# The state update of block 1 moved from step 8 to step 7, and half of the second raw weights loaded in the place of a w load

## The chip, the cores and the metric

The kernel runs on one core of one Trainium2 chip. The metric is device microseconds of one execution, the median of the runs shown. A profile is one further execution, with its own time.

## The reference

Two layers stand one behind the other. The first is an RWKV-6 attention over 4 batches, 8 heads, 768 time steps and a head width of 48. For each head a 48x48 state is carried along time:

```python
for t in range(S):
    kt, vt, rt, wt = (k[:, :, t], v[:, :, t], r[:, :, t], w[:, :, t])
    cur = np.einsum('bhd,bhe->bhde', u[None] * kt, vt)
    y[:, :, t] = np.einsum('bhd,bhde->bhe', rt, state + cur)
    state = wt[:, :, :, None] * state + np.einsum('bhd,bhe->bhde', kt, vt)
```

The second is a dense block on the 3072 tokens of 384 features that come out: `h = x @ w_in` (384 to 2048), `g = h - tanh(h)`, `out = g @ w_out` (2048 to 384), in 32-bit floats.

## The kernel before

The 3072 tokens are cut into eight blocks of 384 (`NB`), two for each batch. A block has six chunks of 64 tokens, and its 8 heads stand as four pairs, worked on in two halves of two pairs (`h1`, pairs 2 and 3, and `h2`, pairs 0 and 1). The recurrence is computed by chunks: products of w forwards (`before`, tile `pre`) and backwards (`behind`, tile `post`), scores within a chunk (`own` and `earlier`, L481), the sums of k and v of each chunk (`update_1`, L562, on TensorE from the turned keys `ks`), the states along the chunks (`update_2`, L574, eleven operations on VectorE for block 1), and the result from states (L664) and scores (L682).

The attention of block 0 is computed in a prologue, `boot`. After it the main loop runs over the blocks, and for each block over 16 steps f (`NF`), one for each 128 of the 2048 hidden features. Step f does the first matmul of block i (`first`, L828, into the PSUM tile hp), copies it on ScalarE (`h`, L831), makes g of it (`slight`, L857 to L861, with `product`, L834), and adds the second matmul of an earlier step (L905 in block 0, three steps behind; L952 in the later blocks). Between these the steps carry the attention of the next block: `plan(i)` says in which step each phase stands (`phases`: TensorE's matmuls, and the VectorE operations that follow them, which are put into the list `behind`) and each preparation (`before`: names such as product_u or held). The order on every engine is the order of the code. For block 0, step f's VectorE work is the list `ops`: conversions, the square, the rest of step f-1, of `behind` the first six, and what is left over waits for the next step.

The phases and block 1's scores share two PSUM tiles, `ps_a.both` (att in the profile), which take turns: turn, update, earlier and the results all use them.

The weights come as raw 64-bit numbers, 16 loads of 768 KB (tile raw, 5 buffers, issued on SP's queue), and are put together as 32-bit floats in four operations: three on ScalarE (L263) and one on VectorE (L267). `boot` converts the first two and most of the third. In block 0 `PIECES[f]` says how many of ScalarE's pieces step f does. `begin_behind(ins, dma)` makes a load wait until an instruction is done. SP issues in order: in `boot` the first raw weights, then w of block 1 for its pairs 2 and 3 (`later.load("w", UP, UP)`), the second raw weights behind the result of the first half, the rows of xT (`fill_holes`), the third and fourth, and w for pairs 0 and 1. At the end of `boot` the first of these w is read by `later.prepare("behind 2")` on VectorE.

Of the kernel before, what the change touches and what calls it, by code (L numbers as in the profile page):

```python
# [38 lines left out]
I32 = mybir.dt.int32  # L39
# [22 lines left out]
UP = 2  # L62
# [3 lines left out]
DM = H * D  # L66
# [6 lines left out]
RAWS = 5  # L73
LAG = 2
LAST = 5
PIECES = 0, 0, 2, 3, 3, 3, 3, 3, 4, 3, 3, 4, 4
UNITS = [(0, 0), (0, 1)] + [u for j in range(NF // 2 - 2) for u in ((1, j), (0, j + 2))] + [(1, NF // 2 - 2),
                                                                                      (1, NF // 2 - 1)]
LATE = 3
# [46 lines left out]
def kernel(  # L126
# [12 lines left out]
    nc = tc.nc  # L139
# [103 lines left out]
    ones = const.tile([P, 1], F32, name="ones", tag="ones")  # L243
    nc.gpsimd.memset(ones, 1.0)

    def load_weights(n, queue):
        part, j = UNITS[n]
        raw = conv.tile([P, 2 * DM, 2], I32, name="raw", tag="raw")
        src = weights[part, j].bitcast(I32).rearrange("p (n two) -> p n two", two=2)
        return part, j, raw, queue.dma_start(out=raw, in_=src)  # L250

    def convert(part, j, raw, _):

# [752 lines left out]
    def plan(i):  # L1006


        formed_w = {}
        if i == 0:  # L1010
            phases = {6: ("turn",), 8: ("update",), 10: ("earlier",), 13: ("result 1",)}
            before = {2: ("behind 0", "take_whole 0"), 3: ("times_behind 2",), 4: ("times_behind 0",),
                      5: ("before 2",), 6: ("before 0",), 7: ("times_before",), 8: ("product_u", "held"), 9: ("bound 2",), 10: ("product_r", "bound 0"),
                      11: ("product_sum",), 12: ("diagonal_in 2", "diagonal_in 0")}
            ahead = {}
            loads = {f: "weights" for f in (0, 1, 3, 4, 5, 6, 7, 8, 9, 10)}
            loads.update({2: "next r", 11: "w", 13: "k", 14: "r"})
            loads = {f: [name] for f, name in loads.items()}
            loads[3] += ["v", "row"]
            loads[4] += ["tokens k"]  # L1020
            loads[9] += ["tokens r"]
        else:
            phases = {3: ("split 2 0",), 4: ("earlier", "split 2 1", "turned 2", "split 0 01"), 5: ("turned 0",),
                      6: ("join 2 0",), 7: ("join 2 1",), 8: ("join 2 2",), 9: ("join 0 02",), 10: ("update",),
                      12: ("result 1",)}
            before = {0: ("times_behind 2",), 1: ("times_behind 0",), 3: ("times_before", "held"),
                      5: ("product_u",), 6: ("product_r",), 7: ("product_sum",), 8: ("diagonal_in 2",),
                      9: ("diagonal_in 0",)}
            ahead = {10: ("bound 2", "bound 0"), 11: ("behind 2", "take_whole 2"), 12: ("behind 0", "take_whole 0"),
                     13: ("before 2",), 15: ("before 0",)}  # L1030
            loads = {1: ["v"], 3: ["tokens k"], 4: ["tokens r"], 7: ["w"], 9: ["k"], 11: ["r"]}
        if i == 1:
            phases = {4: ("split 2 0",), 5: ("split 2 1", "turned 2"), 6: ("split 0 01",),
                      7: ("earlier", "turned 0", "join 2 0"), 8: ("join 2 1",), 9: ("join 2 2", "join 0 01"),
                      10: ("join 0 2",), 11: ("update",), 13: ("result 1",)}
            before = {0: ("behind 2", "take_whole 2", "bound 2"), 1: ("behind 0", "take_whole 0"),
                      2: ("times_behind 2",), 3: ("before 2", "bound 0"), 4: ("times_behind 0",), 5: ("before 0",),
                      6: ("times_before", "held"), 7: ("product_u",),
                      9: ("product_r", "product_sum", "diagonal_in 2"), 10: ("diagonal_in 0",)}
            ahead = {12: ("bound 2",), 13: ("behind 2", "take_whole 2"), 14: ("bound 0",)}  # L1040
            loads = {1: ["v"], 4: ["tokens k"], 6: ["tokens r"], 9: ["w"], 11: ["k"], 12: ["r"]}
            formed_w = {2: (0, 1), 7: (2, 3, 4, 5), 9: (6,), 10: (7, 8), 11: (9,), 12: (0, 1), 13: (2, 3, 4, 5, 6),
                        14: (7, 8, 9)}
        elif i == 2:
            phases.update({3: (), 4: ("split 2 0",), 5: ("earlier", "split 2 1", "turned 2", "split 0 01"),
                           6: ("turned 0", "join 2 0")})
            before = {0: ("behind 0", "take_whole 0", "times_behind 2"), 1: ("times_behind 0",), 2: ("before 2",),
                      3: ("before 0",), 4: ("times_before", "held"), 5: ("product_u",), 7: ("product_r",),
                      8: ("product_sum",), 9: ("diagonal_in 2", "diagonal_in 0")}
            loads = {1: ["v"], 3: ["tokens k"], 5: ["tokens r"], 8: ["w"], 10: ["k"], 11: ["r"]}  # L1050
        return phases, before, ahead, loads, formed_w
# [3 lines left out]
    manual.enter_context(tc.manual_schedule(engines={PE, SP, DVE, ACT}))  # L1055
    raws = []

    def more_weights(queue):
        raws.append(load_weights(more_weights.n, queue))
        more_weights.n += 1  # L1060
        return raws[-1][-1]

# [22 lines left out]
    def boot(ps, pair, blk, later):  # L1085
        h1, h2 = HALVES
        blk.tiles["w"] = states0
        for name, p0, n in (("w", h1 + 1, 1), ("w", h1, 1), ("k", h1, UP), ("r", h1, UP), ("w", h2, UP)):
            blk.load(name, p0, n)
        blk.load_v(h1, UP)  # L1090
        blk.load("k", h2, UP)
        blk.load_v(h2, UP)
        blk.load("r", h2, UP)

        both = (h1, h1 + 1), (h2, h2 + 1)
        blk.behind(h1 + 1, 1)
        blk.behind(h1, 1)
        blk.take_whole(h1, UP)
        blk.totals_by_column(h1)
        nc.scalar.copy(out=later_ident, in_=ident)  # L1100
        blk.before(h1, UP)
        blk.times_behind(h1, UP)
        blk.times_u(h1, UP)
        own = blk.own(ps, h1, ahead=8, late=7)
        blk.turn_1(ps, h1)
        blk.times_before(h1, UP)
        earlier = blk.earlier(ps, h1)
        begin_behind(blk.opened, more_weights(nc.sync))
        later.load("w", UP, UP)
        blk.behind(h2, UP)  # L1110
        blk.take_whole(h2, UP)
        first_a, first_b = convert(*raws.pop(0))
        own()
        blk.turn_2(h1)
        blk.totals_by_column(h2)
        blk.update_half(pair, h1)
        blk.times_behind(h2, UP)
        blk.times_u(h2, UP)
        blk.turn_1(ps, h2)
        blk.turn_2(h2)  # L1120
        earlier()
        blk.results(ps, halved=True)
        blk.result("from_scores", both[0])
        run(blk.states_half(h1))
        blk.result("from_states", both[0], True)
        begin_behind(blk.done, more_weights(nc.sync))
        blk.before(h2, UP)
        own = blk.own(ps, h2)
        blk.update_half(pair, h2)
        updated = blk.done  # L1130
        blk.times_before(h2, UP)
        blk.result_out((3,), nc.scalar.copy)
        blk.result_out((2,))
        earlier = blk.earlier(ps, h2, ahead=2)
        run(first_a)
        blk.fill_holes([nc.sync, nc.gpsimd])
        begin_behind(updated, more_weights(nc.sync))
        more_weights(nc.sync)
        later.load("w", 0, UP)
        second_a, second_b = convert(*raws.pop(0))  # L1140
        third_a, third_b = convert(*raws.pop(0))
        run(second_a)
        more_weights(nc.sync)
        own()
        onwards = blk.states_half(h2)
        blk.results(ps, halved=True)
        busy(blk.yp[0][:, 0], 3)
        blk.result("from_states", both[1])
        earlier(1, 1)
        earlier(0, 1)  # L1150
        later.load("k")
        more_weights(nc.sync)
        for p in reversed(both[1]):
            blk.result("from_scores", (p,), True, more=True)
        run(onwards)
        run(first_b)
        blk.result_out((1,), nc.scalar.copy)
        blk.result_out((0,), nc.vector.tensor_copy)
        run(third_a[:2])
        run(second_b)  # L1160
        later.prepare("behind 2")
        later.prepare("take_whole 2")
        blk.held(0, NPAIR)
        return [(third_a[2], third_b)]
# [32 lines left out]
    for i, blk in enumerate(blocks):  # L1197
# [9 lines left out]
        for f in range(NF):  # L1207
# [22 lines left out]
            elif now == 1:  # L1230
                ops = rest + square + converting(pieces, 3)
            elif not i:
                ops = extra + square + rest[:1] + behind[:6] + spare + rest[1:]
            elif forming:
                ops = between(rest, forming[:2]) + square + formed + forming[2:]
                ops = (between(ops, behind) if len(behind) > 2 else ops + behind) + spare
# [3 lines left out]
                ops = between(rest + formed, behind + spare)  # L1240
            for op in ops:
                op()
            rest, behind, formed, forming, held_back = later_ops, [] if i else behind[6:], [], held_back, []
            extra = [] if i else made_up
            if f < few[i]:
                q = f // 2
# [153 lines left out]
```

## Time and profile before

| | |
|---|---|
| median of 3 runs | 556.11 us (556.03 to 556.36) |
| the profiled execution | 554.57 us |
| its span, first to last instruction | 552.9 us |
| TensorE busy | 537.1 us (97%) |
| VectorE busy | 459.1 us (83%) |
| ScalarE busy | 403.9 us (73%) |
| mean granted TensorE clock | 0.996 |
| `boot`, up to the first L828 | 0 to 24.4 us |
| block 0's 16 steps on TensorE | 24.4 to about 97 us |

The times in the profile count from the first instruction of the span. In its rows a line such as L574 is the line of the kernel file; PE is TensorE, PEld its weight load, DVE VectorE, ACT ScalarE, POOL GpSimd, SP the engine that issues loads. In a list of waits, a row gives who waited for whom, the sum in us, how often, and the longest. In the chain of waits, a row gives start, length and the engine and line that the end of the program hung on. In a timeline, a row gives start, length, engine, line, operation, out<-in and count, and in brackets idle time before it and what ended it. In the list of DMA issues, the last number is the time from issue to landing. A matmul of 32-bit floats stands as two records.

### The profile page before, as it was taken

Reading aid. Unit: us, or ns where it says so; the run is one execution under the profiler, and the core shown is the slowest. Engines: PE = TensorE matmul, PEld = TensorE weight load, DVE = VectorE, ACT = ScalarE, POOL = GpSimd, SP = SyncE. Lnnn points to the kernel's source line nnn. Section 1 sums busy time; section 2 is a strip of 40 time slices with the busy share of each in tenths; the row PEclk is TensorE's granted clock in tenths of the full one; section 3 lists DMA queues with packets and bytes.
Section 4 is the critical chain, followed back from the end, with each engine's and each line's share of the span. In section 5 each row is a group of like instructions: output and inputs, shape, how many; then the busy total and the mean of one; then the engine's idle time right before and its main releaser. Section 6 shows DMA issues by size and latency. Waiting matters only on the chain.

```text
span 552.9 us, 13991 instructions
## 1 busy us (share of the span) xinstructions
PE 537.1 (97%) x5644; PEld 401.5 (73%) x5644; DVE 459.1 (83%) x942; ACT 403.9 (73%) x814; POOL 5.3 (1%) x33
## 2 busy tenths in 40 slices
PE   6899799999999999999999999999999999999996
PEld 3656566677777787878778787777878787787874
DVE  7899979899988899789897799869797897557563
ACT  5799966898668886588766886588865885666561
POOL 1100000000000000000000000000000000000000
PEclk9999999999999999999999999999999999999999
DMA  7898614243302632135211732126222420100101
GB/s 237 300 410 293 218 59 126 87 116 87 117 12 85 107 116 93 59 96 143 82 55 46 142 116 63 52 87 159 61 94 58 91 55 3 56 0 1 43 2 46
DMA packets 53461, 56.29 MB, mean 102 GB/s; under 512 B 21520, under 2 KB 51344, under 8 KB 53392
## 3 DMA queue, kind: packets, MB, share of 16 engines
q1 hardware_dynamic: 53008, 55.18, 33.4%
q8 instruction: 45, 0.74, 0.6%
q14 instruction: 24, 0.20, 0.1%
q10 hardware_dynamic: 288, 0.10, 0.1%
q0 software_dynamic: 96, 0.07, 0.0%
HBM read 44.73 MB, written 4.72 MB: 89 GB/s over the span
## 4 chain that ended last, share of the span: by engine, by line
PE 90%; DVE 3%; ACT 3%; DMA 1%; issue 1%; PEld 0%; PEldq 0%; DVEq 0%; SPq 0%
PE hp L828 43%; PE acc L952 26%; PE att L952 6%; PE acc L905 4%; PE att L481 2%; PE att L664 2%; PE att L682 2%; PE acc L930 2%; PE att L562 2%; ACT up L263 1%; DMA raw<-in_weights 1%; DVE post L417 1%; ACT w_sb L263 1%; DVE states L574 0%; DMA states<-in_wT 0%
## 5 line engine op out<-in xcount | busy, mean ns | idle before, releaser
L828 PE MATMUL hp<-xT,w_sb 128*128 128x384 f32 x750 | 263.8, 488 | 0.5 <-ACT xT L716 0.3
L828 PEld LDWEIGHTS hp<-xT,w_sb 128*128 128x128 f32 x750 | 134.0, 190 | 72.1 <-ACT xT L716 0.9
L831 ACT ACTIVATE h<-hp 128x384 f32<-128x384 f32 x125 | 61.2, 490 | 104.7 <-PE hp L828 104.6
L952 PE MATMUL acc<-forms,g 128*128 128x128 f32 x954 | 133.6, 276 | 0.5
L952 PEld LDWEIGHTS acc<-forms,g 128*128 128x128 f32 x954 | 121.6, 192 | 10.3 <-issue 1.2
L834 DVE SCALAR_TENSOR_TENSOR h<-h,s 128x384 f32<-128x384 f32 x128 | 70.6, 552 | 53.8 <-ACT s L849 53.8
L875 DVE TENSOR_TENSOR g<-g 128x256 f32<-128x256 f32 x265 | 103.2, 418 | 7.9 <-PE acc L952 7.2
L850 ACT ACTIVATE qa<-s,shift 128x384 f32<-128x384 f32 x113 | 69.6, 616 | 3.7
L852 ACT ACTIVATE junk<-s,shift 128x384 bf16<-128x384 f32 x113 | 67.7, 600 | 0.0
L834 DVE SCALAR_TENSOR_TENSOR g<-qa,h 128x384 f32<-128x384 f32 x112 | 61.6, 550 | 1.7 <-ACT qa L860 0.2
L849 ACT ACTIVATE s<-h 128x384 f32<-128x384 f32 x113 | 59.1, 523 | 3.5
L952 PEld LDWEIGHTS acc<-w_sb,g 128*128 128x128 f32 x318 | 46.7, 191 | 9.7 <-ACT sums L920 0.3
L952 PE MATMUL acc<-w_sb,g 128*128 128x128 f32 x318 | 53.1, 276 | 0.1
L952 PE MATMUL att<-w_sb,g 128*128 128x128 f32 x212 | 35.5, 275 | 0.0
L905 PE MATMUL acc<-w_sb,sums 128*128 128x384 f32 x96 | 34.9, 499 | 0.2
L952 PEld LDWEIGHTS att<-w_sb,g 128*128 128x128 f32 x212 | 31.1, 192 | 5.3
L987 DVE TENSOR_TENSOR sums<-sums 128x256 f32<-128x256 f32 x84 | 32.8, 407 | 1.7 <-ACT sums L964 1.5
L263 ACT ACTIVATE up<-raw 128x768 f16<-128x768 f32 (+1 forms) x32 | 33.1, 1066 | 0.0
L905 PEld LDWEIGHTS acc<-w_sb,sums 128*128 128x128 f32 x96 | 18.1, 194 | 13.1 <-DVE sums L834 0.8
L405 DVE TENSOR_TENSOR_SCAN pre<-w,start 128x780 f32<-128x780 f32 x14 | 25.0, 1783 | 0.5
L417 DVE TENSOR_TENSOR_SCAN post<-w,seed 128x780 f32<-128x780 f32 x14 | 24.8, 1774 | 0.0
L852 ACT ACTIVATION_READ_ACCUMULATOR junk<-s,shift 128x1 f32 x113 | 21.1, 187 | 0.0
(113 smaller groups left out, 517.0 us busy)
## 6 DMA issues: line engine op xcount, KB each, us to landing
raw<-in_weights SPq DMA_DIRECT2D x16, 768.0 KB, 5.6
k<-in_kT SPq DMA_DIRECT2D x7, 768.0 KB, 4.6
r<-in_rT SPq DMA_DIRECT2D x7, 768.0 KB, 4.6
w<-in_wT SPq DMA_DIRECT2D x6, 780.0 KB, 4.5
v_sb<-in_v SPq DMA_DIRECT2D x7, 576.0 KB, 3.9
k<-in_tokens SPq DMA_DIRECT2D x7, 576.0 KB, 3.9
r<-in_tokens SPq DMA_DIRECT2D x7, 576.0 KB, 4.9
out_y<-sums SPq DMA_DIRECT2D x18, 128.0 KB, 1.9
```

Of the source, the lines that this page charges most:

```text
L263: return lambda: nc.scalar.activation(out=to, in_=of, func=AF.Copy, scale=scale, bias=bias)
L417: return nc.vector.tensor_tensor_scan(out=back(t[:, 0:width]), data0=back(self.tile("w")[:, a:a + width]), data1=back(seed[:, 0:width]), i ...
L828: nc.tensor.matmul(hp, lhsT=w_in_sb[:, f, kc, :], rhs=xT[kc], start=(kc == KC - 1), stop=(kc == 0))
L831: return h, nc.scalar.activation(out=h, in_=hp, func=AF.Copy, scale=1.0 / UPSCALE)
L834: return lambda: nc.vector.scalar_tensor_tensor(out=out, in0=in0, scalar=scalar, in1=in1, op0=op0, op1=ALU.mult)
L849: nc.scalar.activation(out=s, in_=h, func=AF.Square)
L850: nc.scalar.activation(out=qa, in_=s, func=AF.Square, bias=shift[:, 4:5])
L852: nc.scalar.activation(out=junk[:, 0:NB], in_=s, func=AF.Relu, bias=shift[:, 5:6], accum_out=excess[:, at:at + 1])
L875: return lambda: nc.vector.tensor_tensor(out=G[:, to:to + 2], in0=two(G, g_at(q, a0), g_at(q, a1)), in1=two(G, g_at(q, b0), g_at(q, b1)), ...
L905: nc.tensor.matmul(acc, lhsT=g[:, j * P:(j + 1) * P], rhs=w_out_sb[:, f, :], start=(f == self.first), stop=(f == NF - 1))
L952: nc.tensor.matmul(to, lhsT=G[:, g_at(q, a), :], rhs=rhs, start=start, stop=stop, skip_group_check=True)
L987: ops.append(lambda op=op, at=at: nc.vector.tensor_tensor(out=at[0], in0=at[1], in1=at[2], op=OPS[op]))
```

## The change

It has two parts.

The first moves the phase "update" of block 1 from step 8 of block 0 to step 7. Its eleven VectorE operations no longer are cut after the sixth but stand together, in step 8 where they were in steps 9 and 10. The preparations product_u and held go from step 8 to step 9. `PIECES` gives step 7 four pieces where it had three, and step 8 three where it had four.

The second is in `boot`. The load of the second raw weights is cut in two halves of 384 KB. The first half is issued right behind the first raw weights, where w of block 1, pairs 2 and 3, was issued; the second half where the whole load was. That w is issued between the third and the fourth raw weights.

```diff
-PIECES = 0, 0, 2, 3, 3, 3, 3, 3, 4, 3, 3, 4, 4
+PIECES = 0, 0, 2, 3, 3, 3, 3, 4, 3, 3, 3, 4, 4
...
-    def load_weights(n, queue):
-        part, j = UNITS[n]
+    def load_part(n, raw, queue, of):
+        src = weights[UNITS[n]].bitcast(I32).rearrange("p (n two) -> p n two", two=2)
+        return queue.dma_start(out=raw[:, of], in_=src[:, of])
+
+    def load_weights(n, queue, of):
         raw = conv.tile([P, 2 * DM, 2], I32, name="raw", tag="raw")
-        src = weights[part, j].bitcast(I32).rearrange("p (n two) -> p n two", two=2)
-        return part, j, raw, queue.dma_start(out=raw, in_=src)
+        return *UNITS[n], raw, load_part(n, raw, queue, of)
...
-            phases = {6: ("turn",), 8: ("update",), 10: ("earlier",), 13: ("result 1",)}
+            phases = {6: ("turn",), 7: ("update",), 10: ("earlier",), 13: ("result 1",)}
...
-                      5: ("before 2",), 6: ("before 0",), 7: ("times_before",), 8: ("product_u", "held"), 9: ("bound 2",), 10: ("product_r", "bound 0"),
+                      5: ("before 2",), 6: ("before 0",), 7: ("times_before",), 9: ("product_u", "held", "bound 2"), 10: ("product_r", "bound 0"),
...
         begin_behind(blk.opened, more_weights(nc.sync))
-        later.load("w", UP, UP)
+        more_weights(nc.sync, slice(0, DM))
...
-        begin_behind(blk.done, more_weights(nc.sync))
+        begin_behind(blk.done, load_part(more_weights.n - 1, raws[-1][2], nc.sync, slice(DM, 2 * DM)))
...
         begin_behind(updated, more_weights(nc.sync))
+        later.load("w", UP, UP)
         more_weights(nc.sync)
         later.load("w", 0, UP)
...
-                ops = extra + square + rest[:1] + behind[:6] + spare + rest[1:]
+                ops = extra + square + rest[:1] + behind + spare + rest[1:]
...
-            rest, behind, formed, forming, held_back = later_ops, [] if i else behind[6:], [], held_back, []
+            rest, behind, formed, forming, held_back = later_ops, [], [], held_back, []
```

More of the change, by code (lines that the diff above doesn't have):

```diff
@@ L1056, with more_weights @@
     raws = []
-    def more_weights(queue):
-        raws.append(load_weights(more_weights.n, queue))
+    def more_weights(queue, of=slice(0, 2 * DM)):
+        raws.append(load_weights(more_weights.n, queue, of))
         more_weights.n += 1
```

## The prediction, made before the changed kernel ran

> **What bounds the kernel now.** I read the page's first part, then the list of waits from 10 to 110 us, then the chain that ended last, and went into the timeline of each engine only where these pointed.
>
> ```profile
> PE 537.1 (97%) x5644; PEld 401.5 (73%) x5644; DVE 459.1 (83%) x942; ACT 403.9 (73%) x814; POOL 5.3 (1%) x33
> ```
> ```profile
> PE att L481 <- DVE states L574: 3.0, 1, 3.0
> ...
> ACT w_sb L263 <- DMA raw<-in_weights: 1.1, 1, 1.1
> ```
>
> TensorE is busy 97% of the span, so what can be won is what still holds it up. The waits name two things that this change touches: one wait of 3.0 us of TensorE for the state update on VectorE (L574), and one of 1.1 us of ScalarE for raw weights. The chain shows what the first one costs.
>
> ```profile
> 66.47 0.37 DVE states L574
> 66.83 0.04 issue
> 66.88 2.53 PE att L481 x96
> 69.41 2.80 PE acc L905 x6
> ```
> ```profile
> 121.75 1.56 PE att L481 x96
> ```
> ```profile
> 54.70 1.22 PE att L562 x80
> 55.92 2.13 PE acc L905 x6
> ```
> ```profile
> 63.90:67.30 3.40, 0.42 (x28) 0.42 (x32) 3.24 (x8) 3.40 (x7) 0.00 (x0) 1.00 0.85 294
> 67.30:70.70 3.40, 3.40 (x86) 2.75 (x78) 3.32 (x5) 1.70 (x3) 0.13 (x2) 0.50 0.33 130
> ```
>
> The scores of step 10 ("earlier", L481) write the two PSUM tiles in which the update's products stand, so they start only when the update's VectorE operations have read them, at 66.88. The two windows (columns: stretch, length, busy time of PE, weight loads, VectorE, ScalarE, GpSimd, granted clock, DMA share, GB/s) show the second half of the price: in the 3.40 us after the idle stretch the granted clock is 0.50. So the 96 score matmuls take 2.53 us where the next block's take 1.56, and the next six L905 records 2.80 where those behind L562 take 2.13. The half clock costs 0.97 + 0.67 = 1.64 us; 3.40 us at half speed is 1.7, which agrees.
>
> **The update, one step earlier and in one piece.** No operation is added or removed on TensorE, VectorE or ScalarE. On TensorE the 40 update matmuls (80 records, L562) move ahead of one L905 group and one L828 group. On VectorE the eleven operations of L574 stand together in step 8, where product_u and held stood, and these two go to step 9; ScalarE does one conversion piece more in step 7 and one fewer in step 8.
>
> ```profile
> 57.56 1.35 DVE L370 TENSOR_TENSOR k<-k,u_row 128x1152 f32<-128x1152 f32 x1
> ...
> 74.70 0.56 DVE L857 CUSTOM_DVE_ANT_0 s<-h 128x384 f32<-128x384 f32 x1 [4.03 <-ACT h L831]
> ```
> ```profile
> L574 DVE TENSOR_TENSOR states<-states,whole 128x192 f32<-128x192 f32 x6 | 2.1, 355 | 0.1
> L574 DVE TENSOR_TENSOR states<-states,att 128x192 f32<-128x192 f32 x5 | 1.8, 354 | 0.3
> ```
>
> On VectorE the update begins where product_u began, at 57.56, and its eleven operations take 2.1 + 1.8 + 0.4 idle = 4.3 us: done at 61.9. TensorE reaches the scores at 66.88 - 3.0 = 63.9 (a little later by the next paragraph). So 2.0 us are left between, the 3.0 us wait goes whole, and with it the half clock. What is late next? VectorE does the same work by step 10; the group that it hands over later is g of step 7, out about 2.8 us later than now, at 62.3, and its reader, the L905 group behind the scores, would begin at 63.9 + 1.6 = 65.5. That is covered with 3 us; were it not, each us more would be a us of TensorE. That VectorE can follow is shown by its own idle time: in before it stands still 4.03 us ahead of 74.70, waiting for the very steps that are now early.
>
> The new wait stands in front of the moved matmuls. They need the two copies of the turned keys (ks, L510) on ScalarE, which lie ahead of them only just.
>
> ```profile
> 50.67 2.10 PE L905 MATMUL acc<-w_sb,sums 128*128 128x384 f32 x6
> ```
> ```profile
> 49.97 1.47 ACT L510 COPY ks<-att 128x768 f32<-128x768 f32 x2
> ```
>
> TensorE is free for them at 50.67, where the L905 group now starts. The first copy ends near 50.7, the second at 51.44. In update_1 sixteen of the 40 matmuls read the first copy alone: 16/40 of 1.22 is 0.49, to 51.2; then a wait to 51.5, and 0.73 for the rest, to 52.2. Without a wait it would be 50.67 + 1.22 = 51.9. The price is **0.33 us**; its ends are 0.05 (the copies come early with the weights, below, and TensorE does not) and 0.85 (all 40 wait for both copies). Queued behind that wait are L905 of step 4 and L828 of step 8, so h of step 8 comes 1.22 + 0.33 us later on ScalarE; the conversion piece pulled into step 7 (one of the L263 rows below, 0.94 to 1.08 us) fills that time. I cost it at nothing; without this cover it is that one piece, about 1 us, which ScalarE would make up in the idle time that follows step 10 now.
>
> **The half load in the boot.** The queue of SP now holds: raw 1, first half of raw 2, then (at the point where all of raw 2 stood) its second half, the rows of xT, raw 3, the first w, raw 4, the second w. One DMA more, and the first w three places later.
>
> ```profile
> 19.77 1.08 ACT L263 ACTIVATE up<-raw 128x768 uint16<-128x768 uint32 x1
> 21.97 0.98 ACT L263 ACTIVATE w_sb<-raw 128x768 f32<-128x768 f32 x1 [1.13 <-DMA raw<-in_weights]
> 22.83 1.99 ACT L263 ACTIVATE up<-raw 128x768 f16<-128x768 f32 x2
> 24.67 0.95 ACT L716 COPY xT<-att 48x384 f32<-48x384 f32 x2
> 25.64 0.94 ACT L263 ACTIVATE w_sb<-raw 128x768 f32<-128x768 f32 x1
> 26.47 1.08 ACT L263 ACTIVATE up<-raw 128x768 f16<-128x768 f32 x1
> 27.57 0.49 ACT L831 ACTIVATE h<-hp 128x384 f32<-128x384 f32 x1
> ```
> ```profile
> 16.67 5.28 DMA raw<-in_weights
> ```
> ```profile
> 11.61 0.34 SPq L250 DMA_DIRECT2D raw<-in_weights  x1
> 11.99 0.44 SPq L357 DMA_DIRECT2D w<-in_wT  x1
> ```
> ```profile
> raw<-in_weights SPq DMA_DIRECT2D x1, 768.0 KB, 4.7
> w<-in_wT SPq DMA_DIRECT2D x1, 390.0 KB, 5.3
> ```
>
> Raw 1 lands at 16.3 and w behind it at 17.3, so some 390 KB are worth 1.0 us in this queue. The first half of raw 2 (384 KB) takes w's place and lands near 17.3; the second lands about 1.0 us before 21.95, at 20.95, where ScalarE is free at 20.85. ScalarE so gains 1.0 of the 1.13 us. Little of it can be lost to the extra issue: 0.34 us of SP, which waits anyway.
>
> ```profile
> 20.17 1.00 SPq L250 DMA_DIRECT2D raw<-in_weights  x2
> ```
> ```profile
> raw<-in_weights SPq DMA_DIRECT2D x1, 768.0 KB, 5.0
> ```
> ```profile
> raw<-in_weights SPq DMA_DIRECT2D x1, 768.0 KB, 6.3
> ```
> ```profile
> 23.28 1.22 PE L682 MATMUL att<-scores,v_sb 64*48 64x64 f32 x48 [0.27 <-PEq L704]
> ```
> ```profile
> 26.61 1.77 DVE L417 TENSOR_TENSOR_SCAN post<-w,seed 128x780 f32<-128x780 f32 x1
> ```
>
> But the gain does not pass on whole. The copy at 24.67 needs half of the L682 matmuls, done at 23.9, so it gains at most 0.7; and the conversion behind it needs raw 3, issued at 20.17 and landed 5.0 us later, at 25.2, where it starts at 25.64 now. I take **0.5 us** (ends 0 and 0.7), from the row of raw 3.
>
> ```profile
> 43.07 0.33 ACT h L831
> 43.41 0.04 issue
> 43.45 2.20 PE hp L828 x6
> ```
>
> From 25.64 up to this point the chain runs over ScalarE and VectorE, and here it passes to TensorE, whose step 6 waits for that h; so the 0.5 us reach TensorE. The moved w lands between raw 3 (25.2) and where raw 4 lands now (20.7 + 6.3 = 27.0), by its 1.0 us near 26.2; its first reader on VectorE stands at 26.61, so 0 is its price (ends 0 and 0.4).
>
> **Sum.** 3.0 (wait) + 1.64 (half clock) - 0.33 (new wait) + 0.5 (boot) = 4.8 us. From step 11 on the chain lies on TensorE, and VectorE, ScalarE and the loads hang on its steps, so all moves together. The profiled execution took 554.57 us with a span of 552.9; it would take 549.8 with a span of 548.1. The median of the runs, 556.11, is 1.54 above that execution; taken off it, **551.3 us**. What a measurement of this kernel can tell from no change is about 0.2%, 1.1 us.
>
> **The rivals.** *The half clock is not in every execution* (0.17). The clock fell in a stretch in which TensorE was still busy 0.42 of 3.40 us, and the idle 3.0 us are shorter than the 3.40; were the stretch cut elsewhere, the two windows would each have held more work, and the timed runs might have had no half clock to lose. Then 4.8 - 1.64 = 3.2: 552.9. Against it: the three runs lie within 0.33 us of each other, so they all had it or none had, and they are slower than the profiled one, not faster. [...]
>
> *The small terms fail* (0.13): the copies of ks come late (0.85) or the boot gains nothing. Then 3.0 + 1.64 - 0.85 + 0.5 = 4.3 or 3.0 + 1.64 - 0.33 = 4.3; both, 3.8: 552.3.
>
> *Nothing moves* (0.04): the change is not what it says, in that VectorE and not the wait sets the pace, and TensorE waits for g behind the scores instead. Speaking for it is VectorE's high share; against it the 4.03 us idle ahead of 74.70. Time 556.1.
>
> *Slower, through the moved w* (0.06). VectorE runs in order; if w lands late, the scan at 26.61 holds the conversions' last operation and g of the first steps behind it, and the start of block 0 shifts with it. It costs one us for each us past 26.6 (less what VectorE later waits), and turns the result from 26.6 + 4.8 = 31.4 on: a landing of over 10.7 us after its issue at 20.7. At 12.5 us, twice what raw 4 took in that place, it is 1.8 us slower, 557.9. Against it: raw 4 there took 6.3.
>
> **How the numbers follow.** Forecast 0.60, rivals 0.17, 0.13, 0.04, 0.06. The low end is 3.0 + 1.7 - 0.05 + 0.7 = 5.35, 550.8, less 0.3 for the spread of the runs: 550.4. The high end takes no half clock, 0.85 at the copies and no boot gain: 3.0 - 0.85 = 2.15, 553.9. This holds the first three cases, 0.9, and leaves some of their tails out. Faster by over 0.2%: 0.60 + 0.17 + 0.13 = 0.90; same 0.04; slower 0.06.
>
> **What would show it.** The wait of L481 for L574 is gone from the list; the first 96 L481 records take about 1.56 us and begin near 63.7 (63.9 + 0.33 - 0.5); the clock is 1.00 in the windows from 60 to 75; a new wait of L562 for ks of 0.2 to 0.4 us stands near 51; the first raw wait of ScalarE is 0.1 or none, and h of step 0 starts near 27.1. I am wrong if TensorE waits as long elsewhere before 90 us, if VectorE waits for w at 26.6, or if the half clock stays.

## The result, and the profile after

| | before | changed |
|---|---|---|
| median (range, runs) | 556.13 us (554.91 to 557.34, 6) | 551.32 us (550.33 to 553.59, 6) |
| profiled execution | 554.57 us | 553.59 us |
| its span | 552.9 us | 551.9 us |
| h of step 0 begins | 27.57 us | 31.05 us |
| from there to block 1's first result matmul (L664, after L666) | 54.24 us | 49.95 us |
| from there to the end of the span | 471.0 us | 470.9 us |

The changed kernel takes 0.9915 of the time, interval 0.9894 to 0.9935: 4.8 us less. The profiled execution of it is the longest of its seven; the half clock described below is the reason, and the median does not hang on it. So the fourth and fifth rows of the table are read apart: the start in `boot`, and the **stretch** that holds everything the first part of the change touches. Line numbers of the changed kernel lie two or three above those of before (L481 is L483, L562 is L564, L574 is L576, L664 is L666, L682 is L684, L831 is L833, L905 is L907).

The chain of waits of the changed kernel (start, length, engine and line):

```profile
53.58 1.35 ACT ks L512 x2
54.93 0.04 issue
54.97 0.93 PE att L564 x48
55.90 2.13 PE acc L907 x6
...
67.71 1.56 PE att L483 x96
69.27 2.13 PE acc L907 x6
```

Where the chain of before ran over VectorE's L574 into scores of 2.53 us and an L905 group of 2.80, it now runs on TensorE alone, 1.56 and 2.13. The same two stretches of 3.40 us as were shown of before (columns as there) say why:

```profile
63.90:67.30 3.40, 3.40 (x12) 1.90 (x10) 3.19 (x8) 3.40 (x5) 0.00 (x0) 1.00 0.60 181
67.30:70.70 3.40, 3.40 (x103) 2.47 (x102) 3.40 (x7) 3.40 (x7) 0.13 (x2) 1.00 0.91 281
```

TensorE has no idle time in the first, and the clock is 1.00 in the second. VectorE's timeline has the update's first and last operation, well ahead of the scores:

```profile
61.48 0.35 DVE L576 TENSOR_TENSOR states<-states,whole 128x192 f32<-128x192 f32 x1
...
65.52 0.36 DVE L576 TENSOR_TENSOR states<-states,whole 128x192 f32<-128x192 f32 x1
```

The new wait is in the list of waits, and in TensorE's timeline it makes the 80 records of the update 1.63 us long where they were 1.22:

```profile
PEld att L564 <- ACT ks L512: 0.8, 2, 0.6
```
```profile
54.27 1.63 PE L564 MATMUL att<-v_sb,ks 64*48 64x48 f32 x80
```

In `boot`, ScalarE's timeline no longer has the wait of 1.13 us for raw weights (the first row begins at once), but another, longer one behind it:

```profile
20.74 0.88 ACT L265 ACTIVATE w_sb<-raw 128x768 f32<-128x768 f32 x1
21.51 1.98 ACT L265 ACTIVATE up<-raw 128x768 f16<-128x768 f32 x2
26.95 0.96 ACT L718 COPY xT<-att 48x384 f32<-48x384 f32 x2 [3.46 <-PE att L684]
27.93 0.89 ACT L265 ACTIVATE w_sb<-raw 128x768 f32<-128x768 f32 x1
28.73 1.05 ACT L265 ACTIVATE up<-raw 128x768 f16<-128x768 f32 x1
31.05 0.49 ACT L833 ACTIVATE h<-hp 128x384 f32<-128x384 f32 x1 [1.26 <-PE hp L830]
```

It waits 3.46 us for the result matmuls, since TensorE's clock is 0.50 for three stretches of 3.41 us in this execution (same columns as above):

```profile
16.57:19.98 3.41, 1.64 (x98) 1.39 (x89) 3.00 (x3) 3.18 (x6) 1.57 (x3) 1.00 0.56 147
19.98:23.39 3.41, 3.41 (x60) 2.06 (x61) 1.79 (x3) 3.41 (x4) 0.13 (x2) 0.50 0.53 182
23.39:26.80 3.41, 3.15 (x83) 2.15 (x84) 1.79 (x5) 0.10 (x1) 0.00 (x0) 0.50 0.99 359
26.80:30.22 3.42, 3.42 (x33) 2.06 (x26) 2.56 (x4) 2.80 (x4) 0.00 (x0) 0.50 1.01 394
```

So the first part of the change did what was summed, 4.29 us of stretch against 3.0 + 1.64 - 0.33 = 4.31. Whether the second does anything, and what the half clock in `boot` has to do with the change, was left to the experiments.

### The profile page after: what moved, and what is told of

It is laid out like the page before. It is cut to its first block, busy times and chain, and to the rows that moved or that the text cites. A ratio compares the mean times of both kernels' runs of the same rounds, so it can differ in the third digit from the quotient of the medians.

```text
span 551.9 us, 13996 instructions
## 1 busy us (share of the span) xinstructions
PE 539.0 (98%) x5644; PEld 402.6 (73%) x5644; DVE 459.5 (83%) x942; ACT 403.7 (73%) x814; POOL 5.2 (1%) x33
## 4 chain that ended last, share of the span: by engine, by line
PE 90%; DVE 4%; issue 2%; ACT 2%; DMA 1%; PEld 1%; SPq 0%; PEldq 0%; DVEq 0%
PE hp L830 42%; PE acc L954 26%; PE att L954 6%; PE acc L907 4%; PE att L684 2%; PE att L483 2%; PE att L666 2%; PE acc L932 2%; PE att L564 1%; DMA r<-in_rT 1%; DVE post L419 1%; DVE w_sb L269 1%; ACT up L265 1%; DVE sums L836 0%; DVE scores L491 0%
## 5 line engine op out<-in xcount | busy, mean ns | idle before, releaser
L833 ACT ACTIVATE h<-hp 128x384 f32<-128x384 f32 x125 | 61.4, 491 | 101.7 <-PE hp L830 101.6
L907 PE MATMUL acc<-w_sb,sums 128*128 128x384 f32 x96 | 34.0, 490 | 0.1
L907 PEld LDWEIGHTS acc<-w_sb,sums 128*128 128x128 f32 x96 | 17.8, 190 | 12.4 <-DVE sums L836 0.6
```

The lines of the kernel that those rows point to most:

```text
L833: return h, nc.scalar.activation(out=h, in_=hp, func=AF.Copy, scale=1.0 / UPSCALE)
L907: nc.tensor.matmul(acc, lhsT=g[:, j * P:(j + 1) * P], rhs=w_out_sb[:, f, :], start=(f == self.first), stop=(f == NF - 1))
```

## The experiments

Two theories stood at the start. The first is the prediction's: the update part brings 4.3 us, through the wait and the half clock behind it, and the boot part 0.5. The rival was that the boot part brings nothing or harms, being answered by another wait. All ratios are to the kernel before, run beside.

| kernel | median us (runs) | ratio, interval | h of step 0 | stretch | clock 0.50 in its profile |
|---|---|---|---|---|---|
| before | 556.13 (6) | 1 | 27.57 | 54.24 | step 10 |
| changed | 551.32 (6) | 0.9915, 0.9894 to 0.9935 | 31.05 | 49.95 | boot, three windows |
| e1 update only | 550.70 (6) | 0.9894, 0.9869 to 0.9918 | 28.62 | 49.94 | none |
| e2 boot only | 556.12 (12) | 1.0001, 0.9983 to 1.0020 | 27.35 | 54.26 | step 10 |
| e3 one piece only | 552.37 (6) | 0.9917, 0.9897 to 0.9937 | 29.26 | 50.66 | boot, one |
| e4 earlier only | 551.49 (5) | 0.9899, 0.9878 to 0.9921 | 28.61 | 50.00 | boot, one |
| e5 filled wait | 554.27 (12) | 0.9966, 0.9947 to 0.9984 | 27.47 | 52.82 | none |
| e6 copies first | 551.06 (6) | 0.9904, 0.9877 to 0.9932 | 28.96 | 49.60 | none |
| e7 before again | 556.47 (1) | | 29.25 | 54.25 | boot, one; step 10 |
| e8 copies first, old boot | 550.94 (6) | 0.9912, 0.9893 to 0.9930 | 28.27 | 49.59 | none |
| e9 changed again | 551.48 (7) | 0.9920, 0.9903 to 0.9936 | 30.99 | 49.99 | boot, three |
| e10 pieces as before | 551.24 (6) | 0.9915, 0.9896 to 0.9934 | 28.48 | 49.92 | none |
| e11 third raw early | 551.53 (6) | 0.9929, 0.9903 to 0.9956 | 29.23 | 49.62 | boot, one |
| e12 the same, old boot | 552.24 (6) | 0.9942, 0.9923 to 0.9961 | 30.12 | 49.60 | boot, one |

The last column leaves out the start, before the first clock record of the trace (at 5.0 to 11.3 us), and the last 0.2 to 3.3 us of the span, which are at 0.50 in all of them. From the first result matmul of block 1 to the end all of these take 470.9 to 471.3 us, so a span is the sum of the two columns and that.

**The two parts apart (e1, e2).** e1 has the change but for `load_weights` and `boot`; e2 has only those.

> The update in step 7 and in one piece, with product_u, held and PIECES as in the change; the boot as before. Theory (the sum: wait 3.0, half clock 1.64, new wait for ks -0.33): 4.3 us faster than before, ratio 0.992; no wait of the scores for the update, 96 score records in 1.56 us, a wait for ks of 0.2 to 0.6 us. Rival A (the half clock is not in the timed runs): 2.7 us. Rival B (the half load carries most of the change): under 2 us.

> The half load and the moved w alone; the update as before. Theory: 0.5 us faster, from ScalarE's raw wait of 1.13 us of which raw 3 and the result matmuls let 0.5 through; the 3.0 us wait and its half clock stay. Rival B: 3 us or more. Rival C (the reordered loads get in the way of other traffic in the boot): 0 to 1 us slower.

The update part alone has the whole stretch, 49.94. The boot part alone has none of it, and its time is that of before within some 1 us either way, so the times cannot tell its forecast of 0.5 us from nothing. In e2 ScalarE's timeline shows the gain and where it went:

```profile
20.62 0.93 ACT L265 ACTIVATE w_sb<-raw 128x768 f32<-128x768 f32 x1
21.43 2.03 ACT L265 ACTIVATE up<-raw 128x768 f16<-128x768 f32 x2
24.46 0.96 ACT L718 COPY xT<-att 48x384 f32<-48x384 f32 x2 [1.00 <-PE att L684]
25.45 0.92 ACT L265 ACTIVATE w_sb<-raw 128x768 f32<-128x768 f32 x1
26.26 1.06 ACT L265 ACTIVATE up<-raw 128x768 f16<-128x768 f32 x1
27.35 0.49 ACT L833 ACTIVATE h<-hp 128x384 f32<-128x384 f32 x1
```

The conversion starts 1.35 us earlier than the 21.97 of before, as meant; the copy behind it then waits 1.00 us for result matmuls and starts 0.21 us earlier, and h of step 0 0.22.

**What in the update part does it (e3, e4).** e3 leaves the phase in step 8 and only puts the eleven operations together; e4 only moves the phase, with its pieces and preparations, and leaves the cut.

```diff
 e3, against before:
-                ops = extra + square + rest[:1] + behind[:6] + spare + rest[1:]
+                ops = extra + square + rest[:1] + behind + spare + rest[1:]
 e4, against before:
-            phases = {6: ("turn",), 8: ("update",), 10: ("earlier",), 13: ("result 1",)}
+            phases = {6: ("turn",), 7: ("update",), 10: ("earlier",), 13: ("result 1",)}
```

> Before, with the update's eleven operations no longer cut after the sixth: all in step 9, the matmuls still in step 8. Theory: the eighth operation, which the scores wait for, ends at 61.5 + 8 x 0.39 = 64.6 in place of 66.8, TensorE is ready at 63.9, so a wait of 0.8 us is left; without half clock the gain is 3.0 - 0.8 + 1.64 = 3.9 us, with it 2.2 us. Rival (the step decides, not the cut): 0 to 1 us.

> The update in step 7 with the rest of that part, but still cut after the sixth operation: six in step 8, five in step 9. Theory: the eighth operation ends near 63.1, before TensorE is there (64.2), so the gain is that of the update part whole, 4.3 us. Rival (both are needed): 1 to 3 us, with a wait of the scores left.

Either alone takes most: 3.58 us of stretch with 0.86 us of wait left (e3), 4.24 with none of the matmuls (e4; their first weight load still waits 0.5 us). The two edits overlap; the earlier phase is enough, and the cut costs nothing once it is there. Neither keeps the half clock behind step 10, though e3 still waits.

**The half clock by itself (e5, e7).** e5 is the kernel before with 32 small matmuls ahead of the scores of step 10, to keep TensorE busy in the wait. They write into free columns of a PSUM bank in which a sum of block 0 stands, and with them the kernel's output is off by a relative 0.14; the count and order of the other work are unchanged.

```diff
+                    if i == 0 and f == 10:
+                        fill(acc[2][:, DM:BANK], 32)
```

> Before, with 32 small matmuls of the identity into unused PSUM columns ahead of the scores of step 10: TensorE is kept at work in the wait, the update and its wait stay. Theory (the half clock is 1.64 us of the loss, in every execution): the scores still start when the eighth update operation is done, but run in 1.56 us and the group behind in 2.13; 1.6 us faster than before. Rival A (no half clock in the timed runs): 0 us in the median. Rival B (the matmuls outlast the wait): slower, with the scores released by TensorE's own queue.

> The kernel before, unchanged, once more, to see whether the half clock behind the wait of step 10 is there in another execution and at another place of the clock's windows. Theory: yes, 54.2 us from h of step 0 to L664 again. Rival (the half clock depends on the execution): 52.6 us.

The two stretches around the wait, first of e5 and then of e7. Those of e5 are its own windows, counted back in steps of 3.413 us (the length of the clock record at 0.50 in before, 67.30 to 70.71) from the fall of its clock at 549.87 us, near the end of the program:

```profile
61.77:65.18 3.41, 3.41 (x36) 2.52 (x35) 3.18 (x8) 3.41 (x7) 0.00 (x0) 1.00 0.87 337
65.18:68.59 3.41, 2.19 (x104) 1.88 (x101) 3.20 (x9) 3.41 (x5) 0.00 (x0) 1.00 0.76 264
```
```profile
65.48:68.89 3.41, 0.39 (x21) 0.32 (x24) 3.34 (x9) 3.41 (x7) 0.00 (x0) 1.00 0.90 285
68.89:72.30 3.41, 3.41 (x94) 2.95 (x84) 3.27 (x6) 1.80 (x4) 0.13 (x2) 0.50 0.38 154
```

The 32 matmuls of e5 run from 63.60 to 65.55 us, and the clock stays 1.00. The chain of e5 has the scores and the group behind them:

```profile
66.77 1.78 PE att L486 x96
68.55 2.13 PE acc L910 x6
```

They take 0.75 and 0.67 us less than the 2.53 and 2.80 of before; together this is the 1.42 us by which the stretch is shorter, although the update comes no earlier. 1.64 was priced, with scores of 1.56; why they take 1.78 here is open. In time e5 is 1.9 us faster than before (0.9 to 2.9 by the interval), near the 1.6 of its theory and not the 0 of its rival A, by which the timed runs have no half clock.

e7 has the half clock again, in another execution, but not with another cut: its wait comes later by as much as its windows do. The window begins where the wait begins in e7 (65.48 and 65.55 us), in before (63.90 and 63.86) and in e2 (63.74 and 63.65). In e5 a window ends at 65.18, within the wait. So its profile alone does not show that the matmuls, and not this cut, kept the clock up; the times of its 12 runs are the better evidence. The half clock is a part of the price of the wait, 1.42 us between these two profiles.

**The pieces of ScalarE (e6, e8, e10).** The new wait for ks was shortened by leaving one conversion piece less ahead of the copies, with the new boot (e6) and the old (e8); e10 puts the pieces back as they were before.

```diff
 e6 and e8, in place of the change's 3, 4, 3 in steps 6 to 8:
+PIECES = 0, 0, 2, 3, 3, 3, 2, 4, 4, 3, 3, 4, 4
 e10:
+PIECES = 0, 0, 2, 3, 3, 3, 3, 3, 4, 3, 3, 4, 4
```

> The changed kernel with one conversion piece moved from step 6 behind the key copies, to step 8 (PIECES 2, 4, 4 in steps 6 to 8): the copies end about 1 us earlier, before TensorE comes to the update matmuls. Theory: the new wait for ks (0.33 us by the prediction) goes and nothing is late instead: from h of step 0 to the result matmuls L664 the profile shows 49.6 us in place of 49.95; timed 0.3 us faster than the change, 5.1 faster than before. Rival: g of step 6 or the weights of a later step come late instead, and the 49.95 stays or grows.

> The kernel with the update part of the change alone (boot as before) and the pieces 2, 4, 4 in steps 6 to 8, as in e6_copies_first, which took 551.06 us (ratio 0.9904). In the profile, from h of step 0 to the first result matmul of block 1: 49.6 us, as there. Theory (the boot part of the change is worth nothing in time, since ScalarE's wait for raw weights only turns into one for the result matmuls): the same median as e6 within 1 us, 551.1, ratio about 0.990. Rival (the boot part is worth its predicted 0.5 us, or costs something where the early copies make raw 3 late): 551.6, or below 550.6.

> The change with the pieces of ScalarE as before (3, 3, 4 in steps 6 to 8 where the change has 3, 4, 3). Prediction's reading (h of step 8 comes 1.5 us later through the moved matmuls, and the piece pulled into step 7 fills that time at no cost; without it the piece falls behind h of step 8 and is made up in idle time): the same stretch of 49.95 us within 0.1, median 551.3. Rival (the piece that now stands in step 8 delays g and so TensorE): up to 1.0 us longer, 50.9, median 552.3.

In e6 the update takes, in TensorE's timeline,

```profile
52.17 1.29 PE L564 MATMUL att<-v_sb,ks 64*48 64x48 f32 x80
```

where before has 1.22 and the changed kernel 1.63, and the stretches of e6 and e8 are 0.35 us shorter than those of the changed kernel and e1. That price of the new wait is real and can be had back. The piece pulled forward into step 7 neither costs nor saves anything (e10: 49.92). In the medians 0.35 us cannot be told apart, and neither can e6 from e8: no worth of the half load is seen there either.

**Why no gain of the boot part is seen (e9, e11, e12).** e9 is the changed kernel once more. e11 is e6 with the third raw weights issued right behind the second half of the second, ahead of the rows of xT; e12 is e8 with the same move.

```diff
 e11, against e6:
         begin_behind(blk.done, load_part(more_weights.n - 1, raws[-1][2], nc.sync, slice(DM, 2 * DM)))
+        more_weights(nc.sync)
...
-        begin_behind(updated, more_weights(nc.sync))
         later.load("w", UP, UP)
-        more_weights(nc.sync)
+        begin_behind(updated, more_weights(nc.sync))
```

> The changed kernel once more. From h of step 0 to the first result matmul 49.95 us as in its first profile, ratio to before about 0.991. Theory (a stretch of half clock in the boot belongs to the execution, not to the change): h of step 0 lies between 27.3 and 31.1, at another place than the 31.05 of the first profile, and the span follows it. Rival (the change brings the half clock into the boot): h of step 0 again near 31, the clock again 0.50 from about 20 to 30 us.

> The changed kernel with the pieces 2, 4, 4, and the third raw weights issued right behind the second half of the second (near 17 us) instead of behind the rows of xT (near 20.5). In the profiles so far the third raw weights landed between 24.9 and 27.05 us, with the old boot (25.1 to 26.4) as with the new, and h of step 0 began 1.9 to 2.4 us behind that in every one without half clock in the boot. Theory (the boot part gained nothing in time because the start hangs on whichever is later, the result matmuls behind TensorE's stall or the third raw weights): ScalarE waits for no raw weights, these land near 23, h of step 0 begins at 26.4 to 27.4 by the length of the stall, and the median falls by 0.5 to 1.2 us against the 551.06 of the same kernel with the old place of the load: 549.9 to 550.6. Rival (the loads share their bandwidth, so that the rows of xT or w of block 1 come as much later): h of step 0 at 28 to 29, median 551.

> The same early third raw weights with the boot as before (w of block 1 behind the first raw weights, the second raw weights whole). Theory: ScalarE still waits about 1.1 us for the second raw weights, and h of step 0 begins near 27.5 (27.4 to 27.9); so the boot part of the change is worth 0.2 to 1.1 us once the third raw weights no longer bound the start, and this kernel's median is that much above the one with both. Rival (the half load is worth nothing at all): the same median within 0.2 us.

What led to e11 is e10's boot, where the third raw weights landed late and the moved w behind them (ScalarE, then VectorE):

```profile
26.58 0.91 ACT L265 ACTIVATE w_sb<-raw 128x768 f32<-128x768 f32 x1 [2.10 <-DMA raw<-in_weights]
```
```profile
27.64 1.78 DVE L419 TENSOR_TENSOR_SCAN post<-w,seed 128x780 f32<-128x780 f32 x1 [1.65 <-DMA w<-in_wT]
```

e11 and e12 took these waits away, and the time did not fall: 551.53 against 551.06, 552.24 against 550.94. The theory that the third raw weights bound the start fell in its numbers: h of step 0 began at 29.23 and 30.12 us where 26.4 to 27.4 and 27.4 to 27.9 were forecast. The forecast for e11's rival, a median of 551, is nearer. The pulled load itself took 6.76 us in e11 and 7.89 in e12 and landed at 24.54 and 25.07 us, not near 23. e12's median is 0.7 us above e11's, within the 0.2 to 1.1 of its theory, but the two intervals overlap, so that shows nothing. e11's profile also has a half clock in `boot`, from 21.27 us. What held up e12 is in TensorE's timeline:

```profile
23.42 0.50 PE L682 MATMUL att<-scores,v_sb 64*48 64x64 f32 x18 [0.27 <-PEq L704]
25.91 1.10 PE L682 MATMUL att<-scores,v_sb 64*48 64x64 f32 x30 [1.99 <-issue]
```

In the middle of the result matmuls TensorE stands for 1.99 us and waits for nothing that the profile shows. At this place the DMA parts of the trace hold one packet, 16 KB, of the queue that the page lists as `q8 instruction` (45 packets and 0.74 MB in before), which in before is in flight from 21.27 to 22.31 us, in e8 from 21.10 to 22.30, and in e12, behind the loads that were pulled forward, from 23.25 to 24.52. The matmuls go on 1.39 us after its end in e12 and 1.52 in e8, where the stall is 0.33. The same holds for the stall in the second half's update, which all profiles have; of the changed kernel:

```profile
19.95 0.34 PE L605 MATMUL acc<-v_sb,ks 64*64 64x48 f32 x1 [1.66 <-issue]
```

The packet there ends at 18.50 (1.45 us ahead), in before at 17.83 with the matmuls going on at 19.33 (1.50), in e10 at 17.54 and 18.91 (1.37). The stall was 0.6 to 1.7 us long over the profiles with the old boot as with the new. In both runs with the third raw weights pulled forward the packet of the result matmuls starts late, at 23.19 us (e11) and 23.25 (e12); in the other twelve profiles it starts at 20.67 to 22.07. That TensorE waits for what this packet brings, and that the pulled load keeps the packet back, is the author's reading of these times. No row names either, and that the half load does the same is not shown, its effect being less than the spread.

## Why the prediction was right or wrong

**The wait, the half clock, the cover: right.** The stretch fell by 4.29 us where the terms gave 4.31. The scores begin 36.6 us after h of step 0 (67.64 less 31.05), where the prediction's 63.9 and 0.33 give 36.66 from 27.57. The update ends 1.8 us ahead of them where 2.0 was worked out.

**The new wait: right, and cheap to avoid.** 0.41 us in the update's records for 0.33 predicted. That ScalarE's extra piece costs nothing is borne out by e10; that one piece fewer ahead of the copies would save the wait was not seen.

**The boot: the term that is not borne out.** For 0.5 us e2 measures 0.22 in its profile and 0.0 (0.9 gain to 1.1 loss, from the ratio's interval) in time, which does not exclude 0.5. In the two profiles of the changed kernel h of step 0 began at 31.05 and 30.99 us, not near the 27.1 that was forecast. The first step held: the second half landed at 20.35 us where 20.95 was predicted, and the wait of ScalarE went. The step that failed is the next, which took the result matmuls (done at 23.9) and the landing of the third raw weights (25.2) from one execution as if they were fixed. In the runs both move by more than the term. The stall of 0.6 to 1.7 us shifts the matmuls, a half clock shifted the copy behind them by 2.5 (26.95 in the changed kernel, 24.46 in e2), and the third raw weights landed 4.4 to 6.5 us after their issue (before 4.97, e1 5.8, e10 6.5). Each of the three is enough to swallow the gain.

**The point, met in part by two errors against each other.** The sum moved the profiled execution to 549.8 us and added the 1.54 us by which the median stood above it. That it then met the median to 0.02 us is in part luck, since neither the 0.5 of the boot nor an unchanged 1.54 is shown. The mean clock that is listed with every run tells more. One window of 3.41 us at 0.50 takes 0.0031 off the mean of 552 us, and the half clock in the last 0.2 to 3.3 us of the span up to 0.003 more. Of the 56 runs of before that were made beside the experiments, 19 have a mean clock of 0.996 or more, with little room beyond the window of step 10; their median is 554.7 us. The other 37, at 0.994 or less, have 556.2. Of the 14 runs of the changed kernel (profiled ones included), the seven at 0.998 or more have a median of 551.3, and so have the 12 that are left without the two at 0.988. Between runs of like clock, the window of step 10 taken off, the gain is thus 3.4 us, less than the stretch's 4.3. The rest of the 4.8 comes from the 37 runs of before at a lower clock. That further windows at half clock make them longer is likely, but only one such execution has a profile (e7, 0.993, with a window in `boot`).

Nor is it shown that all of these windows go with the wait. With the wait (before, e2, e7) 28 of 69 runs are at 0.991 or less; without it (all but e3 and e5) 6 of 55 are at 0.994 or less, which is the same limit without the window of step 10. With the limits 0.003 higher, at 0.994 and 0.997, it is 47 and 34. So runs with some two further windows are rarer without the wait, and for those with one no clear difference is seen. The prediction had neither the loss nor this gain in it.

What the loss is, the profiles without half clock in `boot` show only in part: h of step 0 begins at 27.35 to 27.57 us in before, e2 and e5, where the update is in step 8, and at 28.27 to 28.96 in e1, e6, e8 and e10, where it is in step 7 and the third raw weights took 5.8 to 6.5 us to land instead of 4.8 to 5.0. No instruction of `boot` differs between before and e1, and in the changed kernel, e4 and e9, where the update is in step 7 too, the third raw weights took 4.4 to 5.2 us, so the place of the update does not decide it. Whether that is chance in seven profiles or has a cause stays open.

**The rivals.** That the half clock is not in every execution holds for one of the 56 runs (mean clock 0.999, 553.63 us, the fastest); of the others the mean clock cannot tell it. The cut of the wait by a window's end, which this rival names, is in none of the three profiles with the wait and without the filling matmuls. An estimate from the traces speaks against it: wherever a window's end cuts the 3.02 us, one of the two windows is idle for at least 1.51 us and so busy for at most 1.90 us, and behind windows with 1.64 to 1.92 us of matmuls the clock did fall in `boot`, though not behind every such window (below). The moved w did come late in a mild form, 1.2 us in e6 and 1.65 in e10, with a landing 6.8 to 7.0 us after its issue, far from the 10.7 that turns the result. In the times it cannot be seen (e6 551.06, e8 550.94 with w at its old place).

**The half clock in the boot.** e9's profile met the number of the rival named for it, h of step 0 near 31 and three windows from 19.8 us, and not mine. The windows lay at the same phase as in the first profile (19.79 and 19.98 us), and the other 12 runs of this kernel did not have it (their mean clock is 0.995 or more, and three windows take 0.009 off it), so it belongs to an execution and a phase. It also goes with the stall in the second half's update: of the seven profiles whose stall was 1.38 us or longer six have the half clock right behind it (e2 has not), and none of the seven with a stall of 1.17 us or less has it there; in e12 it stands behind the stall of 1.99 us instead. With the old boot e3, e4, e7 and e12 have one such window, and 9 of the 56 runs of before, the window of step 10 included, have a mean clock as low as 0.988. Whether the half load makes three of them likelier than one is not settled.

**A better version.** e6 and e8 have the shortest stretch, 49.6 us. e8 needs no edit of the boot. In time neither can be told from the change itself.

## What to carry to other kernels

Here a wait of 3.0 us of the busiest engine cost more than its length, 1.42 us more by e5 against before, as the clock was 0.50 for 3.41 us behind it; behind the 0.86 us of e3 it stayed 1.00. So price the wait, then look at the granted clock in the stretch behind it. A gain in a stage where three things end within a microsecond of each other is worth the smallest distance among them in the worst execution, so take several profiles before it is counted. Where two edits serve one wait, try each alone: here the earlier start would have been enough.

## What the runs showed of the hardware

**The clock fell behind stretches of 3.4 us in which TensorE was partly busy.** Stretches of 3.4 us with 0.39, 0.42 and 0.48 us of matmuls were followed by a clock of 0.50 (e7, before, e2), and so were stretches with 1.64 us (above) and 1.92 us (e4). After 2.19 us (e5, above; before, in `boot`) it stayed 1.00. Busy time alone does not decide it: after 1.68 us (before, near the start) and 1.97 us (e10) it stayed 1.00 as well. First two stretches of before, then one of e10, then two of e4:

```profile
5.86:9.27 3.41, 1.68 (x7) 0.60 (x7) 3.38 (x4) 1.17 (x3) 0.00 (x0) 1.00 1.04 365
```
```profile
16.08:19.49 3.41, 2.19 (x121) 1.94 (x114) 3.38 (x3) 2.76 (x5) 1.57 (x3) 1.00 0.55 184
```
```profile
32.57:35.98 3.41, 1.97 (x6) 0.87 (x5) 2.46 (x7) 3.41 (x6) 0.00 (x0) 1.00 1.05 431
```
```profile
16.49:19.90 3.41, 1.92 (x106) 1.66 (x98) 3.05 (x3) 3.09 (x6) 1.57 (x3) 1.00 0.53 190
19.90:23.32 3.42, 3.42 (x61) 1.79 (x53) 2.13 (x4) 2.23 (x4) 0.13 (x2) 0.50 0.88 229
```

In before the clock records begin at 5.86, 67.30, 70.71 and 551.99 us, 18, 1 and 141 times 3.413 us apart, and in the changed kernel at 6.32, 19.98, 30.22 and 549.04, 4, 3 and 152 times. None of the stretches named above that a clock of 0.50 followed was wholly idle. In the profiled executions of the changed kernel it stayed at 0.50 through windows with 3.41 and 3.15 us of matmuls, up to 10.24 us.

**TensorE stood still at two places of the boot, until 1.2 to 1.5 us after a packet.** In 14 profiles 17 stalls of it, 0.3 to 2.0 us long, ended 1.2 to 1.5 us after a 16 KB packet of the queue that the page lists as `q8 instruction`, and the packet that started later (e12) went with the longer stall. That TensorE waited for what the packet brought is read from these times; no row says so.
